# Pooled attention between MLP matmuls: scores in 64x64 PE tiles, AV in 64-row tiles, four bursts a batch, k and v loaded by halves of 64 partitions

## The chip, the cores and the metric

The kernel runs on one core of one Trainium2 chip. The metric is the time of one execution on the device in microseconds (us), as the median of several executions. A ratio below is computed as the mean time of one kernel's fast runs over the mean time of the other's fast runs in the same rounds on the same chip, so it is not quite the ratio of the medians that are quoted. An execution is called disturbed, and left out of the ratios, when it is more than 1.5% above the fastest of the same kernel.

Engine names in the profile: PE is TensorE (matmuls), PEld its weight loads, DVE is VectorE, ACT is ScalarE, POOL is GpSimd, SP is SyncE. SPq and ACTq are those engines' sequencers, which also issue DMAs. A DMA "lands" when all its data has arrived. Its landing is told by a semaphore, a counter on which the instructions that need the data wait.

## The reference

```python
def _attn_ref(q, k, v):                       # each 8 x 8 heads x 576 x 64, float32
    k_p = k.reshape(B, H, 72, 8, D).mean(axis=3)     # 576 keys pooled to 72
    v_p = v.reshape(B, H, 72, 8, D).mean(axis=3)
    scores = scale * np.matmul(q, k_p.transpose(0, 1, 3, 2))
    attn = softmax(scores)                    # cut: max, exp, sum
    return np.matmul(attn, v_p)
def _moe_ref(x, w_in, w_out):                 # x: 4608 x 512; w_in 512 x 2048; w_out 2048 x 512
    h = x @ w_in
    g = h - np.tanh(h)
    return g @ w_out
# reference(): x is the attention output with heads side by side, then the MLP
```

## The kernel before

The MLP dominates. Its 4608 rows are done in nine groups of 512: `mlp_h` (h = x w_in, 64 matmuls of 512 columns) and then `mlp_o` (64 more). The attention of batch b+1 is put between the `mlp_o` matmuls of group b, so for six groups (the "stream") TensorE alternates between the two. Batches 0 and 1 are done in the start of the program.

A head has 72 pooled keys, so two heads make 144 rows: 128 go on the partitions of one tile, 16 are left over. K and v come in as raw rows of 8 x 64 floats (2 KB), are pooled by POOL, and k is transposed by a DMA.

```python
def load_main(src, dst, b, t0, t1):           # 128 partitions, four tiles, 1 MB
    return nc.sync.dma_start(out=dst[:, t0:t1, :], in_=src[b, 0:128, t0:t1, :])

def score_mms(b, t, dst, c0, c1, ...):        # two heads in one matmul: KB is block-diagonal
    ... nc.tensor.matmul(dst[p : p + w], lhsT=KB[b % 2][:, o : o + w], rhs=qTs[b][:, m, c0:c1], ...)

def av_half(b, blk, half, x_sb, alloc):       # three matmuls of 130 columns, 128 rows
    for n in range(3): ...
        nc.tensor.matmul(..., lhsT=E[:, t, c0 : c0 + 128], rhs=vb[:, s0 : s0 + 2, :], ...)

for g in range(1, NG):                        # the stream
    for i in range(NHID):
        mlp_h(g, i, gts)
        ...                                   # i == 0: POOL pools k and v of batch nb
        if i == (3 if g == 1 else 8):
            k_dma_transpose(nb); k_place(nb, nc.gpsimd.tensor_copy)
            load_k(nb + 1); load_v(nb + 1); load_q(nb + 1)      # all on one queue, SP's
    for tb in range(4):
        for qd in range(4):
            mlp_o(g, tb, qd * 4, qd * 4 + 4, gts)               # four o_ps matmuls
            u = tb * 4 + qd
            if 1 <= u <= NT: scores(nb, u - 1)
            if u in (7, 8, 9, 10, 12): av(nb, ..., True)        # x goes to xT by DMA transposes
            if u == 12: q_cast(nb + 1); q_dma_transpose(nb + 1)
```

The first `mlp_h` matmul of group b+1 needs xT (x transposed) of batch b+1, which is written by the DMA transposes of that batch's AV.

The softmax here doesn't subtract the row's maximum and nothing guards it: scores larger than these inputs give would overflow.

## Time and profile before

| | before |
|---|---|
| median, in the first rounds | 301.89 us (300.75 to 302.37, 4 runs) |
| span of the profiled run | 299.1 us |
| PE busy | 97% |
| granted TensorE clock | 1.00 |
| first stream group starts | 54.98 us |
| a streaming batch | 30.80 us |
| bytes moved by DMA | 49.79 MB |

The page's view by engine, the stretches of the stream and the order of instructions are shown in the prediction.

### The profile page before, as it was taken

To read this page: it belongs to the slowest core of one execution; us is meant where nothing else is said; L and a number is where in the kernel's file an instruction comes from. 1 tells how busy PE (TensorE), PEld (TensorE's weight loads), DVE (VectorE), ACT (ScalarE), POOL (GpSimd) and SP (SyncE) were. 2 spreads that over 40 slices of the span, in tenths; PEclk is the share of its full clock that TensorE was granted. 3 is DMA by queue.
4 is the path that set the end of the run, shared out by engine and by line. 5 is a ranking of instruction groups with operands and counts; after the bars stand their busy time and mean duration, and the time that the engine had idled before them with its cause. 6 is when DMAs were issued, how large, how long until landed. Compare 5 with 4: busy or idle time off the path is not lost.

```text
span 299.1 us, 4694 instructions
## 1 busy us (share of the span) xinstructions
PE 291.5 (97%) x1671; PEld 142.5 (48%) x1671; DVE 159.1 (53%) x343; ACT 149.4 (50%) x283; POOL 115.5 (39%) x110
## 2 busy tenths in 40 slices
PE   7989999999999999999999999999999999999994
PEld 3454455544544454445444554455445544444443
DVE  5658665673547444753476247716680758108600
ACT  4647583666146633654265516650665166126511
POOL 8500904871496109922971089307940000000000
PEclk9999999999999999999999999999999999999999
DMA  7999999849854998699648974897431430111032
GB/s 251 226 211 278 311 227 310 263 87 328 234 113 99 271 297 134 117 302 245 107 88 235 300 167 94 242 294 159 97 66 35 95 92 0 37 70 36 0 72 70
DMA packets 66183, 49.79 MB, mean 166 GB/s; under 512 B 39920, under 2 KB 52976, under 8 KB 66160
## 3 DMA queue, kind: packets, MB, share of 16 engines
q1 hardware_dynamic: 58832, 42.94, 56.0%
q0 software_dynamic: 4752, 4.72, 9.4%
q10 hardware_dynamic: 2576, 1.84, 2.3%
q8 instruction: 13, 0.21, 0.3%
q14 instruction: 10, 0.08, 0.1%
HBM read 36.70 MB, written 9.44 MB: 154 GB/s over the span
## 4 chain that ended last, share of the span: by engine, by line
PE 85%; DMA 9%; POOL 4%; issue 0%; SPq 0%; ACT 0%; DVE 0%; POOLq 0%
PE o_ps L456 40%; PE hT_ps L428 37%; DMA w1b<-in_moe_w_in_dram 4%; PE x_ps L346 4%; DMA k_raw<-in_k_dram 4%; PE s_ps L298 3%; POOL k_raw L198 1%; DMA out_dram<-o_sb 1%; POOL k_raw L203 1%; POOL kd L206 1%; POOL w2b L510 0%; PE xT_ps L390 0%; POOL v_raw L576 0%; PE qT_ps L171 0%; POOL w1b L503 0%
## 5 line engine op out<-in xcount | busy, mean ns | idle before, releaser
L456 PE MATMUL o_ps<-w2b,gT 128*128 128x512 bf16 x560 | 134.4, 380 | 0.0
L441 DVE TENSOR_TENSOR gT<-hT_ps,t_sb 128x512 bf16<-128x512 f32 x144 | 98.9, 691 | 57.7 <-ACT t_sb L439 57.6
L428 PE MATMUL hT_ps<-xT,w1b 128*128 128x512 bf16 x576 | 126.9, 379 | 0.3 <-ACT xT L397 0.3
L439 ACT ACTIVATE t_sb<-hT_ps 128x512 f32<-128x512 f32 x144 | 85.6, 597 | 38.3 <-PE hT_ps L428 37.5
L428 PEld LDWEIGHTS <-w1b 128*128 128x128 bf16 x576 | 55.9, 98 | 66.5 <-issue 0.4
L456 PEld LDWEIGHTS <-gT 128*128 128x128 bf16 x560 | 52.5, 98 | 52.0 <-issue 1.4
L465 ACT COPY o_sb<-o_ps 128x512 f32<-128x512 f32 x33 | 19.3, 585 | 75.2 <-PE o_ps L456 75.2
L359 DVE RECIPROCAL rden<-x_ps 128x4 f32<-128x4 f32 x80 | 14.2, 177 | 52.5 <-PE x_ps L346 52.0
L360 DVE TENSOR_TENSOR x_sb<-x_ps,rden 128x256 bf16<-128x256 f32 x80 | 34.0, 425 | 3.5 <-DMA xT<-x_sb 0.6
L148 POOL CAST q_bf<-q_raw 128x2048 bf16<-128x2048 f32 x6 | 11.3, 1888 | 59.9 <-issue 34.8
L198 POOL TENSOR_TENSOR k_raw<-k_raw 128x1280 f32<-128x1280 f32 x7 | 20.2, 2886 | 27.4 <-DMA k_raw<-in_k_dram 16.6
L317 ACT ACTIVATE E<-s_ps 128x288 bf16<-128x288 f32 x60 | 21.4, 410 | 13.2 <-PE s_ps L298 13.0
L346 PE MATMUL x_ps<-VB,E 128*128 128x130 bf16 x240 | 20.8, 221 | 0.4 <-ACT xT L397 0.3
L346 PEld LDWEIGHTS <-E 128*128 128x128 bf16 x240 | 16.9, 98 | 8.8 <-DVE VB L230 0.6
L216 POOL TENSOR_TENSOR v_raw<-v_raw 128x1280 f32<-128x1280 f32 x6 | 17.4, 2898 | 0.0
L298 PE MATMUL s_ps<-qT,KB 128*128 128x288 bf16 (+5 forms) x128 | 17.0, 290 | 0.2
L298 PEld LDWEIGHTS <-KB 128*128 128x128 bf16 (+1 forms) x128 | 7.0, 96 | 10.2 <-issue 3.5
L527 PE MATMUL warm_ps<-xT 128*128 128x512 bf16 x29 | 10.2, 465 | 1.3 <-DVE xT L539 1.3
L206 POOL TENSOR_TENSOR kd<-k_raw 128x640 bf16<-128x640 f32 x7 | 10.8, 1540 | 0.5
L203 POOL TENSOR_TENSOR k_raw<-k_raw 128x640 f32<-128x640 f32 x7 | 10.8, 1541 | 0.5
L397 ACT CAST xT<-xT_ps 128x256 bf16<-128x256 f32 (+1 forms) x14 | 5.8, 436 | 8.5 <-PE xT_ps L390 5.1
L219 POOL TENSOR_TENSOR v_raw<-v_raw 128x640 f32<-128x640 f32 x6 | 9.3, 1544 | 0.5
(73 smaller groups left out, 100.7 us busy)
## 6 DMA issues: line engine op xcount, KB each, us to landing
k_raw<-in_k_dram SPq DMA_DIRECT2D x7, 1024.0 KB, 5.9
q_raw<-in_q_dram SPq DMA_DIRECT2D x7, 1024.0 KB, 10.2
v_raw<-in_v_dram SPq DMA_DIRECT2D x7, 1024.0 KB, 9.3
out_dram<-o_sb SPq DMA_DIRECT2D x38, 128.0 KB, 2.4
out_dram<-o_sb SPq DMA_DIRECT2D x16, 256.0 KB, 3.7
w1b<-in_moe_w_in_dram POOLq DMA_DIRECT2D x4, 512.0 KB, 14.2
w2b<-in_moe_w_out_dram POOLq DMA_DIRECT2D x4, 512.0 KB, 16.9
k_raw<-in_k_dram SPq DMA_DIRECT2D x7, 128.0 KB, 5.8
```

The lines of the kernel that those rows point to most:

```text
L198: first = eng.tensor_tensor(out=r[:, :, 0:4, :], in0=r[:, :, 0:4, :], in1=r[:, :, 4:8, :], op=ALU.add)
L216: eng.tensor_tensor(out=r[:, :, 0:4, :], in0=r[:, :, 0:4, :], in1=r[:, :, 4:8, :], op=ALU.add)
L298: nc.tensor.matmul(dst[p : p + w], lhsT=KB[b % 2][:, o : o + w], rhs=qTs[b][:, m, c0:c1], start=True, stop=True,)
L317: nc.scalar.activation(out=E[:, t, half * hs : (half + 1) * hs], in_=ps[:, :], func=ACT.Exp, scale=SCALE)
L346: nc.tensor.matmul(ps[:, 2 * n : 2 * n + 2, :].rearrange("p h d -> p (h d)") if n < 2 else ps.rearrange("p (a s) d -> p a s d", s=2)[:, :, ...
L359: nc.vector.reciprocal(out=rden[:, :, :], in_=ps[:, :, D:D1])
L360: nc.vector.tensor_tensor(out=x_sb[:, half, :, :], in0=ps[:, :, 0:D], in1=rden[:, :, :].to_broadcast([128, 4, D]), op=ALU.mult,)
L428: nc.tensor.matmul(h_tiles[i][:, :], lhsT=w1b[:, fb, i * 128 : (i + 1) * 128], rhs=xT[:, fb, tok0 : tok0 + TG], start=(fb == 0), stop=(fb ...
L439: nc.scalar.activation(out=t_sb[:, :], in_=h_ps[:, :], func=ACT.Tanh)
L441: nc.vector.tensor_sub(out=gT[:, :], in0=h_ps[:, :], in1=t_sb[:, :])
L456: nc.tensor.matmul(o_ps[:, :], lhsT=gts[i][:, tb * 128 : (tb + 1) * 128], rhs=w2b[:, i, :], start=(i == 0), stop=(i == NHID - 1),)
L465: (nc.vector.tensor_copy if g == 0 and tb % 2 else nc.scalar.copy)(out=o_sb[:, :], in_=o_ps[:, :])
```

## The change

The intent: block-diagonal k wastes half of each score matmul on zeros, and AV multiplies with masked v. In tiles of the PE array (64x64 for scores, 64 rows x 128 columns for AV) four or two small matmuls run at a time and nothing is multiplied by zero. Since a change of tile shape costs time, the small matmuls are grouped in four bursts a batch (before: ten), which needs six PSUM banks at once. For the tiles the layout of pooled k and v must be: head pair's first head on partitions 0 to 63, second on 64 to 127. So k and v are loaded by two DMAs of 64 neighbouring partitions each.

```diff
-    def load_main(src, dst, b, t0, t1):
-        return nc.sync.dma_start(out=dst[:, t0:t1, :], in_=src[b, 0:128, t0:t1, :])
+    def load_half(src, dst, b, i, ts=slice(0, NM), eng=nc.sync):
+        return eng.dma_start(out=dst[64 * i : 64 * i + 64, ts, :], in_=src[b, i, :, ts, :])
+
+    def load_main(src, dst, b):
+        return [load_half(src, dst, b, i) for i in range(2)]
 ... (cut: banks by hand, left-over rows in one load, masks)
+    def score_main(b, j, dst, c0, c1):
+        for s, i in ((0, 0), (1, 1), (0, 1), (1, 0)):
+            m = j + 2 * i
+            nc.tensor.matmul(
+                dst[s][64 * i : 64 * i + 64],
+                lhsT=kTs[b][64 * s : 64 * s + 64, m, 64 * s : 64 * s + 64],
+                rhs=qTs[b][64 * s : 64 * s + 64, m, c0:c1],
 ... (cut)
+    def av_mms(b, blk, pss):
+        mms = [(pss[i][:, t, :], i, t, vb[64 * i : 64 * i + 64, t, :])
+            for t in range(NM) for i in range(2)
+        ] + [...]                                   # one more pair, 260 columns, left-over rows
+        for n, (dst, i, t, rhs) in enumerate(mms):
+            nc.tensor.matmul(dst, lhsT=E[64 * i : 64 * i + 64, t, c0 : c0 + 128], rhs=rhs, ...)
 ... (cut: the start, reordered for scores of four heads at once)
-                    if 1 <= u <= NT:
-                        scores(nb, u - 1)
-                    if u in (7, 8, 9, 10, 12):
-                        av(nb, (7, 8, 9, 10, 12).index(u), ps_b1, True)
+                    if u in (2, 5):
+                        scores_pairs(nb, u // 3)
+                    if u in (7, 10):
+                        av_stream(nb, (0, 1, 2) if u == 7 else (3, 4))
```

## The prediction

> **What bounds the kernel now.** I read the page first, then the busy time of each engine over chosen stretches, then the instructions in order of time, at last the list of waits. The page says that TensorE is busy 97% of the span, and that its two MLP lines make most of the chain that ended last:
>
> ```profile
> PE 291.5 (97%) x1671; PEld 142.5 (48%) x1671; DVE 159.1 (53%) x343; ACT 149.4 (50%) x283; POOL 115.5 (39%) x110
> ...
> L456 PE MATMUL o_ps<-w2b,gT 128*128 128x512 bf16 x560 | 134.4, 380 | 0.0
> L428 PE MATMUL hT_ps<-xT,w1b 128*128 128x512 bf16 x576 | 126.9, 379 | 0.3 <-ACT xT L397 0.3
> L346 PE MATMUL x_ps<-VB,E 128*128 128x130 bf16 x240 | 20.8, 221 | 0.4 <-ACT xT L397 0.3
> ```
>
> To be seen: the idle time before the MLP groups (last column) is nothing, while DVE, ACT and POOL are about half idle. A busy sum is not yet a limit, so I compared one streaming batch (an MLP group with the attention of the next batch put between its o_ps matmuls) with an MLP group at the end that has no attention in it:
>
> ```profile
> 85.95:116.75 30.80, 30.80 (x175) 15.07 (x174) 16.68 (x36) 15.36 (x30) 13.73 (x12) 1.00 0.86 202
> 116.75:147.56 30.81, 30.81 (x176) 15.05 (x174) 16.68 (x36) 15.36 (x30) 19.11 (x16) 1.00 0.77 186
> 239.98:267.61 27.63, 27.63 (x130) 12.50 (x128) 11.07 (x16) 11.89 (x20) 0.00 (x0) 1.00 0.16 50
> ```
>
> The columns are the stretch, its length, then busy time of PE, PEld, DVE, ACT, POOL, the clock, the DMA share and GB/s. The difference, 30.80 - 27.63 = 3.17 us, is all that attention costs on TensorE in one of the six streaming batches. 6 x 3.17 = 19.0 us is the whole pot for the stream. In order of time, where that 3.17 goes in one batch:
>
> ```profile
> 73.84 0.41 PE L298 MATMUL s_ps<-qT,KB 128*128 128x288 bf16 x2
> 74.09 1.03 PE L456 MATMUL o_ps<-w2b,gT 128*128 128x512 bf16 x4
> 75.04 0.43 PE L298 MATMUL s_ps<-qT,KB 128*32 128x288 bf16 x8
> 75.41 1.90 PE L456 MATMUL o_ps<-w2b,gT 128*128 128x512 bf16 x8
> 77.14 0.51 PE L346 MATMUL x_ps<-VB,E 128*128 128x130 bf16 x6
> 77.49 1.03 PE L456 MATMUL o_ps<-w2b,gT 128*128 128x512 bf16 x4
> ```
>
> First column start, second duration with the last one's latency. What counts is start to start. One o_ps matmul takes 0.216 us. Two score matmuls of 288 columns take 0.25 (73.84 to 74.09), six AV matmuls of 130 columns 0.35 (77.14 to 77.49). The left-over scores (8 matmuls in 32-column tiles) take 0.46: four o_ps matmuls from 74.09 would have ended their stream at 74.95, and the next starts at 75.41. Sum: 4 x 0.25 + 0.46 + 5 x 0.35 = 3.2, the 3.17 found above.
>
> The left-over scores are the one place before where tiles are used. In the single records four of them start within 10 ns (75.044 to 75.054), the other four 123 ns later, so four tiles do run as one. But the first starts 310 ns after the o_ps matmul ahead of it (not 216), and the next o_ps 219 ns after the last of them (not some 120). So one change of tile shape costs about 0.095 us, in and out alike.
>
> The third place is the start of the program, up to 55 us, where TensorE is not always the bound:
>
> ```profile
> 30.21 2.90 POOL L198 TENSOR_TENSOR k_raw<-k_raw 128x1280 f32<-128x1280 f32 x1 [16.58 <-DMA k_raw<-in_k_dram]
> ...
> 36.23 1.54 POOL L206 TENSOR_TENSOR kd<-k_raw 128x640 bf16<-128x640 f32 x1
> ...
> 37.82 0.45 PE L259 MATMUL kT_ps<-ident,kd 128*128 128x128 bf16 x5 [0.52 <-POOL kd L206]
> ```
>
> POOL waits 16.6 us for k of batch 1, pools it, and TensorE waits (0.5 us; its weight load 1.0) for the result. So TensorE's own start (the MLP's h matmuls run without a break from 20.4) is already as fast as that chain lets it be, bar about half a microsecond.
>
> **What the Trainium skill says.** "TensorEngine Tiling (Array Packing)", Key Properties: changing the tiling mode drains TensorE; the trace agrees, 0.095 us each way. "TensorE: Matmul & The Clock Gate", Part 3: matmuls in different tiles start some 4 ns apart and finish as one; the trace agrees for 32-column tiles (2 to 5 ns). The same page, Weight-path perf modes: the fast weight load wants 128 weight columns. Before, N = 64 matmuls that each load 128 columns follow each other 28 to 30 ns apart, so such a load takes no more than that; nothing before shows 64-row or 64x64 tiles. "DMA: Bandwidth & Descriptors", Queues: engines take turns between queues; so splitting a load into two on one queue adds no bandwidth.
>
> **The change part by part.** From the built order of the changed kernel, a streaming batch has four bursts between o_ps matmuls instead of ten.
> - Main scores: 8 matmuls of 128x288 become 16 in 64x64 tiles, four at a time: 4 x 0.123 = 0.49 in place of 1.0.
> - Left-over scores: the same 8 matmuls, 2 x 0.123 = 0.25.
> - AV: per block six matmuls of 130 columns (0.35) become four pairs of 65 columns and one pair of 260, each pair in two 64-row tiles. A pair of 65 columns takes at least 0.03 (the N = 64 pace above), the 260 one 260/512 x 0.216 = 0.11: 0.23 a block if pairs run as one, 0.35 if the two weight loads follow each other (0.06 a pair). The latter is no gain at all. I take 0.25.
> - Changes of shape: two before. After: burst 1 has three (in, 64x64 to 32 columns, out), the others two each: nine, 9 x 0.1 = 0.9 in place of 0.2.
>
> Sum after: 0.49 + 0.25 + 5 x 0.25 + 0.9 = 2.89 against 3.17: **0.28 us saved a batch, 1.7 us for six**. All of it is on the path, since TensorE is idle nowhere in that stretch.
>
> What moves beside it. ACT: ten exponentials of 288 columns (410 ns each) become five of 576 (about 0.65 by the step from 410 at 288 to 597 at 512), so 4.1 to 3.3 us. DVE: ten reciprocals of 177 and ten products of 425 ns become five pairs of some 0.2 and 0.69, 6.0 to 4.5 us. POOL: placing k and one wide mask go. All of these engines are half idle, so this is worth nothing in itself. Six banks a burst can make waits, so I checked the tightest: AV's first burst needs the exponentials of burst 2, 2 x 0.65 + some 0.3 after TensorE leaves, and eight o_ps matmuls (1.73) lie between. Just enough.
>
> Start. Whole-block AV (four times 0.2 + 0.69 on DVE instead of eight times 0.6), no copy of v's left rows by POOL, and scores of four heads per load should make the MLP's first matmuls start some 2 us earlier than now (an estimate from the rows of DVE: 19.6 now). But w1 and k of batch 1 come over DMA engines that are saturated (share 1.24 between 10 and 20 us), and the same bytes are wanted. K of batch 1 is issued when the second piece of w1 lands (18.7), lands at 30.05, and POOL needs 7.7 us for it. POOL issues w1 perhaps 0.5 us sooner. So the 2 us turn into a longer wait at the k transpose near 37 us, and about **0.4 us** is left.
>
> Batch 1 and the end of batch 0 use AV block by block with two changes of shape each: 0.25 + 0.2 against 0.35, so six times +0.1, less 0.2 for the scores: **+0.4 us**, of which the part in batch 0 goes into the wait.
>
> Sum: -1.7 - 0.4 + 0.3 = -1.8, so 302.1 - 1.8 = **300.3 us**.
>
> **Rivals.** (a) The bursts save nothing: row tiles with a 128-column weight load each don't pair up, AV stays at 0.35 a block, and the changes of shape eat the scores' gain. Then a batch costs 0.49 + 0.25 + 1.75 + 0.9 = 3.39, 6 x 0.22 = +1.3 us, and 303 us in all. For it: no 64-row tile was seen before. Against it: 32-column tiles load their weights 3 ns apart. I give it one chance in five. (b) The start does get faster: smaller loads by halves make k of batch 1 or w1 land earlier, and the 2 us count in full: 298.5. For it: less on the queues' issue (v's left rows in one load, not four). Against: saturated DMA, and loads of 64 partitions that fill from one queue may rather be slower. One in six. (c) Waits: the exponentials or the norms don't end in time for the next burst, some 0.3 us a batch: 302. The lists of waits before have no TensorE wait at all between 60 and 240 us, and the new order leaves slack everywhere but in one place. (d) Transfers in the stream: k and v split in two and landing later. They have many microseconds of slack there (k of the next batch lands at 72, and is pooled from 85.95 on), so nothing.
>
> **Range and chances.** AV's pace moves the result by +2.5 or -0.6 us, the start by +1 or -2, waits by +1.5. Low 298.4, high 302.9. Faster by over 2% needs 296.1 us, a saving of 6.0: stream and start together at their best give some 4.5. Slower by over 2% needs a stall of one microsecond in every batch. So 0.03, 0.94, 0.03.
>
> **What would show it.** A streaming batch of 30.5 us in place of 30.80; three to five tenths between o_ps matmuls at the second burst, 0.8 at the first, about 0.95 at the third; four score matmuls starting within some 15 ns; AV pairs about 30 ns apart (60 would be rival a). h matmuls from about 17 to 18 us, and a wait of 2 to 3 us at the k transpose of batch 1 near 37.5. Wrong it would be if that transpose starts before 36 or after 39, if TensorE waits inside a batch for ACT or DVE, or if a pair of AV matmuls takes over 45 ns.

## More of the kernel before

From the page of the kernel before, the queue that carries the loads and the median time of its loads from issue to landing:

```profile
q1 hardware_dynamic: 58832, 42.94, 56.0%
...
k_raw<-in_k_dram SPq DMA_DIRECT2D x7, 1024.0 KB, 5.9
q_raw<-in_q_dram SPq DMA_DIRECT2D x7, 1024.0 KB, 10.2
v_raw<-in_v_dram SPq DMA_DIRECT2D x7, 1024.0 KB, 9.3
```

Columns of the first line: packets, megabytes, and the time those packets took as a share of 16 engines' span. Then the same kernel's stretches from the first MLP matmul to the stream, and over the four middle streaming batches:

```profile
18.49:54.98 36.49, 35.65 (x252) 18.73 (x252) 23.68 (x54) 23.23 (x43) 13.44 (x8) 1.00 1.12 275
85.78:209.01 123.23, 123.23 (x697) 60.23 (x696) 66.70 (x144) 61.42 (x120) 63.30 (x51) 1.00 0.80 195
```

After the engines' busy times come the clock, the DMA share and GB/s. (A share above 1 means that packet durations overlap.) In the start the DMA engines are full, at 1.12. In the stream they are at 0.80 on average.

## The result

| | before | after |
|---|---|---|
| median | 301.89 us (4 runs) | 329.77 us (329.60 to 331.58, 4 runs) |
| ratio | | 1.0943, 95% interval 1.0893 to 1.0993 |
| span of the profiled run | 299.1 us | 327.9 us |
| granted TensorE clock | 1.00 | 0.969 |
| first stream group starts | 54.98 us | 63.18 us |
| six streaming batches | 184.84 us | 205.82 us |
| from there to the end | 59.3 us | 58.9 us |

The result is correct and 9.4% slower. The predicted time was 300.3 us, and the range ended at 302.9. The last three rows split the 28.8 us by which the span grew: +8.2 in the start, +21.0 in the stream, -0.4 at the end.

The page after, the lines of engines, the clock and DMA by slice, and the chain that ended last:

```profile
PE 296.9 (91%) x1881; PEld 135.9 (41%) x1916; DVE 148.2 (45%) x270; ACT 145.2 (44%) x251; POOL 105.7 (32%) x96
...
PEclk9799979999796999989999999999999999999999
DMA  7999999984998599969995899479963162021023
...
PE 67%; DMA 23%; SPq 3%; issue 2%; POOL 2%; DVE 1%; ACT 1%; POOLq 0%
PE PS L477 34%; PE PS L506 28%; DMA q_raw<-in_q_dram 11%; DMA xT<-x_sb 7%; DMA w1b<-in_moe_w_in_dram 4%; PE PS L377 2%; PE PS L308 1%; SPq L127 1%; DMA out_dram<-o_sb 1%; PE PS L318 1%; ACT q_bf L166 1%; SPq L133 1%; DVE x_sb L412 0%; POOL v_raw L127 0%; SPq L293 0%
```

PE was 97% busy and is now 91%. The chain was PE 85% and is now PE 67%, DMA 23%. In the chain, `q_raw` loads have 11% and the transposes of x 7%; neither was among the first entries before. The clock dips in some of the slices in which PE idled or just after them, not in all.

The MLP groups of the same page, and the DMA lines that answer to those of before:

```profile
L477 PE MATMUL PS<-xT,w1b 128*128 128x512 bf16 (+1 forms) x586 | 129.9, 379 | 15.0 <-DMA xT<-x_sb 13.0
L506 PE MATMUL PS<-w2b,gT 128*128 128x512 bf16 x537 | 128.4, 385 | 2.3 <-issue 1.6
...
q1 hardware_dynamic: 59040, 43.07, 64.6%
...
k_raw<-in_k_dram SPq DMA_DIRECT2D x14, 512.0 KB, 7.3
v_raw<-in_v_dram SPq DMA_DIRECT2D x14, 512.0 KB, 9.8
q_raw<-in_q_dram SPq DMA_DIRECT2D x5, 1024.0 KB, 15.4
```

The matmuls themselves are a little slower: told apart by shape, those of 512 columns take 387 and 385 ns, and 379 and 380 before. (The 379 in the first line is a mean with 40 shorter ones in it.) The h matmuls have 15 us of idle time before them where they had 0.3, and 13.0 of it ended with a transpose of x. The queue moves 43.07 MB instead of 42.94, but its packets take 64.6% of a longer span instead of 56.0%. A load of 512 KB of k now lands after 7.3 us; one of 1024 KB landed after 5.9 us. The q loads of 1024 KB are what they were before, and land after 15.4 us instead of 10.2: they are issued on the same queue behind k and v.

The stretches after, from the start of one h phase to the next:

```profile
22.36:63.18 40.82, 37.64 (x301) 19.59 (x306) 22.89 (x52) 22.78 (x43) 10.75 (x7) 0.96 1.09 204
63.18:103.04 39.86, 32.18 (x201) 13.98 (x203) 15.94 (x27) 15.12 (x26) 14.56 (x13) 0.92 0.90 192
103.04:138.09 35.05, 32.33 (x198) 14.08 (x203) 15.29 (x26) 14.75 (x25) 14.84 (x12) 0.94 0.89 170
138.09:171.60 33.51, 31.99 (x199) 14.03 (x203) 15.29 (x26) 14.75 (x25) 15.14 (x12) 0.95 0.94 178
171.60:204.37 32.77, 30.39 (x199) 13.62 (x204) 15.29 (x26) 14.75 (x25) 13.68 (x12) 1.00 0.89 179
204.37:238.45 34.08, 30.39 (x199) 13.61 (x203) 15.29 (x26) 14.75 (x25) 14.29 (x11) 1.00 0.89 174
238.45:269.00 30.55, 30.23 (x199) 13.71 (x204) 15.29 (x26) 14.17 (x24) 12.63 (x10) 1.00 0.44 85
103.04:238.45 135.41, 125.11 (x793) 55.35 (x809) 61.14 (x104) 58.99 (x100) 57.95 (x44) 0.97 0.90 175
```

The first five streaming batches take 33 to 40 us at a DMA share of 0.89 to 0.94. The sixth, which has no further batch to load (share 0.44), takes 30.55: 0.25 less than before. So the change is worth on PE what was predicted, wherever the loads let it. In the start, the share of 1.09 is much that of before (1.12), but it moved 204 GB/s instead of 275.

How a slow load becomes a PE wait is seen in the chain of the longest one, in order of time (start, duration, what):

```profile
83.77 0.62 SPq L133
84.39 0.04 issue
84.43 15.36 DMA q_raw<-in_q_dram
99.86 3.04 DMA xT<-x_sb
102.90 0.14 issue
103.04 1.01 PE PS L477 x2
```

The q load is issued at 84.43, at the end of the row of k and v loads, and takes 15.36 us. The transpose of x that the profile chains to it is issued at 99.86, though the norms that feed the transposes had all started by 94.2. In the trace's instruction records the two use the same semaphore (number 104), and SP waits on it before it issues the later one. So x doesn't need the data of q: the transpose waits for q because semaphores are used again in turn. It lands at 102.90, and 0.14 us later the first h matmul of the next group starts, 5.3 us late.

The packets behind this, from the trace: on that queue, a packet of 2 KB (a row of k or v, or of the output) had a median duration of 84 ns before and has 154 ns after (means 107.1 and 146.9, over 12,992 and 12,800 packets).

**What page of the Trainium skill bears on it.** The page "SBUF — State Buffer", section "Door 1: The DMA port swizzle (why `[64,N]` ≈ `[32,N]`)", says that partitions 0 to 63 reach only 8 of 16 ports to SBUF and 64 to 127 the other 8; it gives 196 GB/s against 328 for a transfer of 1 MiB, a factor of 0.60. The packets are near it: 84/154 = 0.55. The prediction had not looked this page up.

### The profile page after: what moved, and what is told of

It is laid out like the page before. It is cut to its first block, busy times and chain, and to the rows that moved or that the text cites. A ratio compares the mean times of both kernels' runs of the same rounds, so it can differ in the third digit from the quotient of the medians.

```text
span 327.9 us, 5052 instructions
## 1 busy us (share of the span) xinstructions
PE 296.9 (91%) x1881; PEld 135.9 (41%) x1916; DVE 148.2 (45%) x270; ACT 145.2 (44%) x251; POOL 105.7 (32%) x96
## 3 DMA queue, kind: packets, MB, share of 16 engines
q1 hardware_dynamic: 59040, 43.07, 64.6%
## 4 chain that ended last, share of the span: by engine, by line
PE 67%; DMA 23%; SPq 3%; issue 2%; POOL 2%; DVE 1%; ACT 1%; POOLq 0%
PE PS L477 34%; PE PS L506 28%; DMA q_raw<-in_q_dram 11%; DMA xT<-x_sb 7%; DMA w1b<-in_moe_w_in_dram 4%; PE PS L377 2%; PE PS L308 1%; SPq L127 1%; DMA out_dram<-o_sb 1%; PE PS L318 1%; ACT q_bf L166 1%; SPq L133 1%; DVE x_sb L412 0%; POOL v_raw L127 0%; SPq L293 0%
## 5 line engine op out<-in xcount | busy, mean ns | idle before, releaser
L477 PE MATMUL PS<-xT,w1b 128*128 128x512 bf16 (+1 forms) x586 | 129.9, 379 | 15.0 <-DMA xT<-x_sb 13.0
L491 DVE TENSOR_TENSOR gT<-PS,t_sb 128x512 bf16<-128x512 f32 x144 | 99.0, 691 | 83.9 <-ACT t_sb L489 83.0
L506 PE MATMUL PS<-w2b,gT 128*128 128x512 bf16 x537 | 128.4, 385 | 2.3 <-issue 1.6
L489 ACT ACTIVATE t_sb<-PS 128x512 f32<-128x512 f32 x144 | 85.9, 599 | 57.1 <-PE PS L477 55.6
L515 ACT COPY o_sb<-PS 128x512 f32<-128x512 f32 x33 | 19.5, 590 | 69.7 <-PE PS L506 69.7
L327 ACT ACTIVATE E<-PS 128x576 bf16<-128x576 f32 (+3 forms) x44 | 23.9, 606 | 28.2 <-PE PS L308 27.3
L412 DVE TENSOR_TENSOR x_sb<-PS,rden 128x512 bf16<-128x512 f32 x30 | 20.8, 692 | 1.0
L575 PE MATMUL PS<-xT 128*128 128x512 bf16 x28 | 10.6, 504 | 1.2 <-DVE xT L587 1.2
L377 PE MATMUL PS<-VB,E 64*128 64x65 bf16 x320 | 11.3, 192 | 0.0
L377 PE MATMUL PS<-VL,E 64*128 64x260 bf16 x80 | 10.2, 268 | 0.1
## 6 DMA issues: line engine op xcount, KB each, us to landing
q_raw<-in_q_dram SPq DMA_DIRECT2D x5, 1024.0 KB, 15.4
```

What stands on the lines that cost most here:

```text
L327: nc.scalar.activation(out=out, in_=in_, func=ACT.Exp, scale=SCALE)
L377: nc.tensor.matmul(dst, lhsT=E[64 * i : 64 * i + 64, t, c0 : c0 + 128], rhs=rhs, start=(n < 2), stop=(n >= len(mms) - 2), skip_group_check ...
L412: nc.vector.tensor_tensor(out=out, in0=ps[:, :, :, 0:D], in1=rden[:, :, :, :].to_broadcast([128, 2, NM, D]), op=ALU.mult,)
L477: nc.tensor.matmul(h_tiles[i][:, c0:c1], lhsT=w1b[:, fb, i * 128 : (i + 1) * 128], rhs=xT[:, fb, tok0 + c0 : tok0 + c1], start=(fb == 0 an ...
L489: nc.scalar.activation(out=t_sb[:, :], in_=h_ps[:, :], func=ACT.Tanh)
L491: nc.vector.tensor_sub(out=gT[:, :], in0=h_ps[:, :], in1=t_sb[:, :])
```

## The experiments

Theory, formed after the result: the loads of 64 neighbouring partitions are the whole of the loss; PE's part of the change is as good as predicted. Rivals: the tiles or bursts cost something that only shows in the stream; splitting a load in two costs, whatever the partitions; the lost clock is a cause of its own; the start alone is at fault.

All medians (those of e3, e5 and e8 have one disturbed run in them; the ratios don't), in the order of their rounds; each ratio is to the kernel before in the same rounds (300.66, 300.76, 300.72 and 300.87 us):

| run | median us | ratio [95%] |
|---|---|---|
| e1 after, full-width loads | 300.56 | 0.9994 [0.9976, 1.0013] |
| e2 before, halves of 64 | 322.00 | 1.0698 [1.0674, 1.0723] |
| e3 before, every other partition | 315.98 | 1.0486 [1.0415, 1.0558] |
| e4 after, halves on two queues | 350.00 | 1.1643 [1.1619, 1.1666] |
| e5 before, halves, stream only | 313.20 | 1.0391 [1.0359, 1.0423] |
| e6 before, every other, stream only | 300.90 | 1.0001 [0.9983, 1.0019] |
| e7 after, full width in the stream only | 307.73 | 1.0229 [1.0194, 1.0265] |
| e8 after, mended | 302.80 | 1.0059 [1.0041, 1.0077] |
| e9 after, idle time filled | 328.10 | 1.0897 [1.0876, 1.0919] |
| e10 e1 without bursts for AV | 304.31 | 1.0125 [1.0104, 1.0147] |
| e11 before, only k in halves, stream | 302.18 | 1.0045 [1.0030, 1.0061] |
| e12 start of before, stream of e8 | 300.06 | 0.9979 [0.9963, 0.9996] |
| e13 before, only v in halves, stream | 303.18 | 1.0076 [1.0050, 1.0103] |
| e14 e5 again, one look | 314.42 | (one run) |

### e1: the changed kernel with full-width loads

The same bytes in the same number of DMAs, but each load has two of the four tiles over all 128 partitions. The rows land in wrong places, so the result is wrong (relative error 1.30). Instructions, sizes and counts are those of the changed kernel.

```diff
     def load_half(src, dst, b, i, ts=slice(0, NM), eng=nc.sync):
-        return eng.dma_start(out=dst[64 * i : 64 * i + 64, ts, :], in_=src[b, i, :, ts, :])
+        return eng.dma_start(out=dst[:, 2 * i : 2 * i + 2, :], in_=flat[b, 0:128, 2 * i : 2 * i + 2, :])
 ... (cut: one tile per load in the start)
```

> The changed kernel with the same number of loads of k and v and the same bytes, but every load over all 128 partitions (two of the four tiles a load, instead of 64 partitions of all four). The rows then lie in wrong places, so the result is wrong on purpose. Theory P (loads into 64 neighbouring partitions move at half the rate, and the late loads hold up everything behind them on the queue): 298 to 303 us, 2 KB packets back at a median near 84 ns (154 in the changed kernel), no wait of TensorE inside a streaming batch, clock back at 1.0. Rival B (the four bursts, the grouped transposes of x or the reuse of banks make the waits): stays at 325 to 332 us.

Measured 300.56 us. The median 2 KB packet is 84 ns again. PE waits nowhere in the stream, as the stretches show (start; first streaming batch; the four middle ones):

```profile
20.07:56.52 36.45, 36.16 (x305) 19.34 (x305) 22.85 (x52) 22.74 (x43) 13.43 (x8) 1.00 1.08 275
56.52:87.07 30.55, 30.55 (x205) 13.69 (x202) 15.92 (x27) 14.51 (x25) 13.53 (x11) 1.00 0.84 200
87.07:209.27 122.20, 122.20 (x810) 54.75 (x808) 61.08 (x104) 58.91 (x100) 59.79 (x46) 1.00 0.78 196
```

Busy time equals the length: 30.55 us a batch. So tiles, bursts and banks are innocent, and the width of the loads is the whole loss of 29 us. This run also lets the prediction's sum for PE be read in one batch (start, duration with the last one's latency, what):

```profile
73.01 0.44 PE L318 MATMUL PS<-qT,kT 64*64 64x288 bf16 x8
73.38 0.43 PE L328 MATMUL PS<-qT,KL 128*32 128x288 bf16 x8
73.74 2.77 PE L516 MATMUL PS<-w2b,gT 128*128 128x512 bf16 x12
76.44 0.44 PE L318 MATMUL PS<-qT,kT 64*64 64x288 bf16 x8
76.81 1.90 PE L516 MATMUL PS<-w2b,gT 128*128 128x512 bf16 x8
78.64 0.30 PE L387 MATMUL PS<-VB,E 64*128 64x65 bf16 x8
78.78 0.27 PE L387 MATMUL PS<-VL,E 64*128 64x260 bf16 x2
78.89 0.29 PE L387 MATMUL PS<-VB,E 64*128 64x65 bf16 x8
...
79.46 2.76 PE L516 MATMUL PS<-w2b,gT 128*128 128x512 bf16 x12
```

As in the prediction, what counts is start to start at 0.216 us an o_ps matmul. The last o_ps before this stretch starts at 72.705 and would have made way at 72.92; the next starts at 73.74, so burst 1 cost 0.82 us. Burst 2 lies between 76.33 (73.74 plus twelve matmuls) and 76.81: 0.48. The third lies between 78.54 and 79.46: 0.92. The fourth, which ends with the o_ps matmul at 82.74, is 0.69. The sum is 2.91 us; predicted was 2.89. A pair of 65-column AV matmuls starts 29 to 39 ns after the last, and its two halves 2 to 5 ns apart.

### e2 and e3: the kernel before with its loads split

e2 splits each main load of the kernel before into two of 64 neighbouring partitions, e3 into two of every other partition. All else stays, results are correct.

```diff
 # e2 (e3: slice(i, 128, 2) in place of slice(64 * i, 64 * i + 64))
-        return nc.sync.dma_start(out=dst[:, t0:t1, :], in_=src[b, 0:128, t0:t1, :])
+        return [
+            nc.sync.dma_start(out=dst[slice(64 * i, 64 * i + 64), t0:t1, :],
+                in_=src[b, slice(64 * i, 64 * i + 64), t0:t1, :])
+            for i in range(2)
+        ]
```

> The kernel before with one thing changed: each main load of k and v (from the SP queue) is two loads of 64 neighbouring partitions. Right result. Theory P: slower, 312 to 330 us, 2 KB packets at a median near 154 ns. Rival B: 302, at most 304 us for the additional issues.

> As the run before, but each of the two loads takes every other partition (0, 2, 4 ... and 1, 3, 5 ...), so again 64 partitions a load. Right result. If it is the ports that a load reaches (theory P as the SBUF page has it): 301 to 304 us and packets near 84 ns. If it is the number of partitions or of loads: as slow as the run before.

Measured 322.00 and 315.98 us (313.92 without its disturbed run), so e3 missed the 301 to 304 us that were expected of it. The packets separate the two cleanly: a median of 154 ns in e2, of 84 in e3. So do the four middle batches of the stream:

```profile
102.40:232.94 130.54, 123.90 (x697) 60.07 (x697) 65.68 (x141) 61.55 (x121) 62.38 (x52) 1.00 0.89 181
```

```profile
99.03:222.25 123.22, 123.22 (x697) 60.29 (x696) 66.61 (x144) 61.42 (x120) 63.61 (x53) 1.00 0.79 195
```

e2 (first) takes 130.5 us there, e3 (second) 123.2, as the kernel before. But both lose in the start, 15.9 and 13.2 us by the first stream group, and e3 has no slow packets. The cause is in ACT's timeline of e2, a line that e3 has too (9.06 us):

```profile
31.67 0.92 ACT L400 CAST xT<-xT_ps 128x256 bf16<-128x256 f32 x3 [9.88 <-DMA k_raw<-in_k_dram]
```

ACT sat idle for 9.88 us, until a k load had landed: its own sequencer stood at the issue of a DMA of q, which waits for a semaphore of a load on the other queue. More loads in flight at the start made that collision. So neither start tells anything of the changed kernel, and both runs were inconclusive there.

### e4: the halves on two queues

If the two halves ran side by side they would fill all ports. The changed kernel, with each second half issued from ACT:

```diff
-        return [load_half(src, dst, b, i) for i in range(2)]
+        return [load_half(src, dst, b, i, eng=(nc.sync, nc.scalar)[i]) for i in range(2)]
```

> The changed kernel with the second half of each streamed k and v load on the ScalarE queue, the first half on SP. Right result. If two halves in flight at once fill both sets of ports: 300 to 312 us. If, as the SBUF page says, two loads can't be fused: within 2% of the changed kernel, 323 to 333 us; a further cost is possible from the issues on ScalarE.

Measured 350.00 us, worse than anything else and outside both expected ranges. The packets of 2 KB stay slow (medians 148 and 144 ns on the two queues). On top, PE waits 22.2 us in the stream for gT, the product of DVE that needs ACT's tanh: ACT is now held at its DMA issues (16.4 us of its waits before tanh end with a DMA). The same page of the skill, section "Can I just issue two DMAs to hit both halves?", says no, with +6% for two at once. This run agrees that it is no remedy, though it doesn't measure that figure.

### e5 and e6: as e2 and e3, but in the stream only

```diff
+        if b < 2:
+            return [nc.sync.dma_start(out=dst[:, t0:t1, :], in_=src[b, 0:128, t0:t1, :])]
```

> The kernel before with only the streamed loads (batch 2 and later) of k and v split into two loads of 64 neighbouring partitions; the start is untouched, because in the two runs before this the split at the start also shifted which load waits for which semaphore and held up ScalarE by 10 us. Right result. Theory P, ports: the streaming part of the earlier run grew by 7.9 us, so 306 to 311 us. Rival, the number of loads: the same as the even and odd run of this call.

> As the run before, with every other partition in each of the two loads. Theory P, ports: 299 to 302 us, as the kernel before. Rival, the number of partitions or of loads: as slow as the run before.

Measured 313.20 (313.01 without its disturbed run) and 300.90 us; 306 to 311 was expected of e5, so the size was missed by 2 us. This is the cleanest pair: the kernel before, correct results, the same number of loads, the same bytes, the same queue. Neighbouring partitions cost some 12 us, every other partition nothing. So "two loads instead of one" is not the cause, and 64 partitions are not either; it matters which 64. The profiled execution of e5 was disturbed (1084 us); its other three runs agree (311.6 to 313.4).

### e7: the changed kernel, full width in the stream only

```diff
+        if b < 2:
+            return eng.dma_start(out=dst[64 * i : 64 * i + 64, ts, :], in_=src[b, i, :, ts, :])
```

(ahead of e1's form; wrong as there.)

> The changed kernel with full-width loads only from batch 2 on, the start as changed (64 neighbouring partitions). Wrong result on purpose. If the loss adds up of the start (stream begins 8.2 us later in the changed kernel, 1.5 us later with full-width loads everywhere) and of the stream: 305 to 310 us. If the backlog of the start is what spoils the stream: over 312 us.

Measured 307.73 us. From the first h matmul to the stream it is as slow as the changed kernel; the middle batches are at full pace:

```profile
22.16:63.49 41.33, 38.17 (x305) 19.74 (x305) 22.88 (x52) 22.76 (x43) 13.41 (x8) 0.96 1.10 238
94.32:216.52 122.20, 122.20 (x808) 54.80 (x809) 61.15 (x104) 58.85 (x100) 59.24 (x45) 1.00 0.81 196
```

The stream starts at 63.49, against 56.52 in e1: the halves cost 7.0 us in the start. The rest, some 22 us (329.8 - 307.7), is the stream. So both parts are due to the same loads, and the start alone was not at fault.

### e9: the idle time filled

In the changed kernel TensorE idles, and the granted clock falls afterwards. To tell whether that adds its own time, dummy matmuls were put where it idles most.

```diff
+                    if g == 1 and u == 2:
+                        warm_pe(9, b0=5)
 ...
+                    if g in (1, 2) and u == 15:
+                        warm_pe(22 if g == 1 else 10, b0=5)
```

> The changed kernel, with idle stretches of TensorE in group 1 and 2 of the first heads filled by dummy matmuls into a bank that is free then. Theory (the loads set the pace and the lost clock is only a companion): the time stays within 1.5 us of the changed kernel's 329.8, the mean granted clock goes up from 0.969. Rival (the clock that falls after the idle stretches adds its own microseconds, about 5 of the 28): about 324 us.

Measured 328.10 us, by the ratios some 1.4 us less than the changed kernel (1.0897 against 1.0943), with the clock at 0.983. The four middle batches:

```profile
103.47:236.97 133.50, 126.69 (x819) 55.92 (x819) 61.11 (x104) 58.98 (x100) 57.80 (x44) 0.99 0.91 178
```

133.5 us, against 135.4, at nearly the same DMA share. The rival's 324 us did not come. But only about half of the lost clock was given back, and 1.4 us is within the intervals of the two ratios, so this run bounds the clock's own part loosely. Another bound: over the six streaming batches PE is busy for 187.52 us in the changed kernel and 183.30 in e1. The slower matmuls are thus worth 4.2 us at most; the rest of the loss there is waiting.

### e11, e13 and e14: how much slow loading the stream can bear

The kernel before, with k alone, v alone, or both in halves of 64 neighbours, from batch 2 on.

```diff
 # e11 (e13: v_pairs in place of k_pairs; e14: without that condition, as e5)
+        if b < 2 or src is not k_pairs:
+            return [nc.sync.dma_start(out=dst[:, t0:t1, :], in_=src[b, 0:128, t0:t1, :])]
```

> The kernel before, with only the k loads of batches 2 to 5 as two loads of 64 neighbouring partitions; v and q as before. With both k and v (and q) so, the stream cost 12 us. Theory (the queue had slack, and the loss begins only once the slower packets fill the queue's whole batch): at most 303 us. Rival (each slow load delays its consumer by itself): near half of the loss, 306 to 307.

> The kernel before, with only the v loads of batches 2 to 5 as two loads of 64 neighbouring partitions. With k alone it was 302.18 (+1.5), with both some +12. Theory (there is a fixed amount of room on the DMA engines, and either tensor alone just fits into it): as with k alone, 302 to 303.5, and a DMA share near 0.87 in the four middle batches. Rival (v is what hurts, because the q load queued behind it is the one that is waited for): 308 to 312, most of the loss.

> Both k and v of batches 2 to 5 by halves of 64 partitions, in the kernel before: one look, because the profiled execution of the first run of this form was disturbed (1084 us) and left no usable trace. Theory (room runs out): about 312 us, DMA share of 0.90 or more in the batches that got longer, each of them ending in a wait of the first MLP matmul for a transposed x. Rival (each load delays its own consumer, with the engines not full): the same time, with a DMA share no higher than with k alone, 0.87.

Measured +1.5, +2.3 and, with both, +12 to +13.6 us. The four middle batches of each, in that order (of e14 also the first streaming batch and the first of the four):

```profile
87.08:210.32 123.24, 123.23 (x696) 60.35 (x697) 66.64 (x144) 60.87 (x119) 64.53 (x53) 1.00 0.87 194
```

```profile
87.55:211.12 123.57, 123.40 (x697) 60.23 (x698) 66.65 (x144) 60.87 (x119) 65.00 (x53) 1.00 0.89 194
```

```profile
54.71:93.12 38.41, 31.14 (x176) 15.02 (x174) 17.31 (x37) 15.73 (x31) 16.29 (x15) 0.98 0.93 199
93.12:126.56 33.44, 33.44 (x175) 15.68 (x175) 16.66 (x36) 14.77 (x29) 16.39 (x14) 0.92 0.85 178
93.12:222.96 129.84, 126.35 (x697) 60.66 (x696) 65.69 (x141) 61.42 (x120) 63.11 (x52) 0.98 0.90 182
```

Length times DMA share is the work of the DMA engines, here for one batch: 24.6 us before (123.23 x 0.80 / 4), 26.8 with k, 27.5 with v, 29.2 with both, and 30.5 in the changed kernel (135.41 x 0.90 / 4). The step from before to both, 4.6 us, is what the packets make of it: two tensors of 512 packets, each 70 ns longer, over 16 engines are 4.5 us. With v alone the share is 0.89 and the batches still take the 30.8 to 30.9 us that PE needs; with either tensor alone, what is lost is lost for the most part in the first streaming batch (32.5 and 32.3 us). With more work the share hardly rises, 0.90, and the batch grows instead, to 129.84/4 = 32.5 us. No streaming batch of these runs or of the changed kernel shows a share above 0.94. So the loss is not k's or v's own: each alone nearly fits, and the two together don't. Both rivals (half the loss with k; v in particular) fall.

Two things in e14 are not as expected. Over half of its loss, 7.6 us, is in the first streaming batch. And one of the four that follow (33.44 us) has no wait of PE at all: PE is busy throughout, at a clock of 0.92 and a DMA share of 0.85. That batch grew by its clock; the other three grew by 1.0 to 1.7 us at shares of 0.90 to 0.92.

### e10: what the bursts are worth

e1 (wrong), with AV of each of the five blocks in a burst of its own: six more changes of shape a batch.

```diff
-                    if u in (7, 10):
-                        av_stream(nb, (0, 1, 2) if u == 7 else (3, 4))
+                    if u in (7, 8, 9, 10, 12):
+                        blk = (7, 8, 9, 10, 12).index(u)
+                        av_stream(nb, (blk,), ((6, 0, 4)[blk % 3],))
```

> The full-width form of the changed kernel (300.56 us; wrong data on purpose), with AV of each block in its own step again, so that a batch has six more changes of tile shape. Theory (a change of shape drains the array and costs about 0.1 us): 6 x 0.1 x 6 batches = +3.6 us, so about 304. Rival (a change of shape costs nothing beside the matmuls; the grouping in bursts buys nothing): 300.6, within 0.6.

Measured 304.31 us. Its batches are 31.18 to 31.19 us, against 30.55: 0.635 us for six changes, 0.106 each. Without the bursts the tiles would be slower than the kernel before (30.80), so the grouping is needed for the change to be worth anything.

### e8: a mended version

If every other partition is as fast as full width, then the changed kernel can keep its tiles: half i of k goes to partitions i, i+2, i+4, ..., score weights are picked with a stride of two, and v is brought into halves by one matmul with a permutation matrix for each batch.

```diff
-        return eng.dma_start(out=dst[64 * i : 64 * i + 64, ts, :], in_=src[b, i, :, ts, :])
+        return eng.dma_start(out=dst[i::2, ts, :], in_=src[b, i, :, ts, :])
 ...
-                lhsT=kTs[b][64 * s : 64 * s + 64, m, 64 * s : 64 * s + 64],
+                lhsT=kTs[b][64 * s : 64 * s + 64, m, s::2],
 ...
+    def v_perm(b, ps):
+        nc.tensor.matmul(ps, lhsT=perm[:, :], rhs=VP[b % 2].rearrange("p t d -> p (t d)"), ...)
+        nc.vector.tensor_copy(out=VB[b % 2][:, :, 0:D], in_=ps.rearrange("p (t d) -> p t d", t=NM))
```

> A mended version with a right result: each half of k and v goes to every other partition (all ports); the score matmuls take every other column of k transposed as weights, and v is brought to 64 neighbouring partitions by one permutation matmul of 256 columns a batch. Theory P: 298 to 303 us (300.6 with full-width loads, and 6 x 0.11 us for the permutation). Rival B: stays above 320 us.

Correct, and 302.62 us in its three undisturbed runs (302.39 to 302.98; the 302.80 above has the disturbed one in it). That undoes all but some 2 us of the loss, but it is 0.6% slower than the kernel before. Its profiled execution was a disturbed one (clock 0.755).

### e12: the start of before, the stream of e8

Batches 0 and 1 and their loads as in the kernel before, the stream as in e8.

```diff
     def load_k(b):
+        if b > 1:
+            return load_wide(k_main, k_raw[b % 2], b) + load_rest(k_left, k_raw[b % 2], b)
 ... (cut: the same for v; scores_pairs, av_stream and v_perm of e8 in the stream loop)
```

> A correct kernel: batches 0 and 1 as in the kernel before (full-width loads, its scores), batches 2 to 5 in the changed form with loads to every other partition and one permutation matmul a batch for v. Theory (the PE side of the change saves 0.25 us a batch, the permutation gives 0.11 back, the start is that of before): 0.5 to 0.9 us less than before, 299.7 to 300.2. Rival (a switch of forms in mid-stream, or the two halves of a load, brings a new wait): 301 or more.

Correct, 300.06 us (six runs), 0.9979 of the kernel before, and the interval ends below 1. Three of its batches:

```profile
55.45:86.10 30.65, 30.65 (x205) 13.79 (x203) 16.35 (x28) 14.51 (x25) 14.74 (x13) 1.00 0.71 206
86.10:116.76 30.66, 30.66 (x204) 13.82 (x203) 15.71 (x27) 14.72 (x25) 14.30 (x11) 1.00 0.79 193
116.76:147.42 30.66, 30.66 (x204) 13.80 (x203) 15.71 (x27) 14.72 (x25) 15.89 (x13) 1.00 0.70 196
```

30.66 us is 30.55 and 0.11 for the permutation, as expected; six of them save 0.84 us, and the stream starts 0.47 us later than before (55.45). The gain is tiny, 0.6 us of 300.7: the interval just excludes no gain.

## Why the prediction was wrong

**The step that failed** is rival (d), "k and v split in two and landing later. They have many microseconds of slack there ..., so nothing", with the sentence under the skill that "splitting a load into two on one queue adds no bandwidth" as the whole account of the loads by halves. What the runs showed in its place: a 2 KB packet to 64 neighbouring partitions takes 154 ns, not 84, and the stream has too little slack for that. It cost 12 to 13.6 us with k and v so loaded in the stream of the kernel before (e5, e14), and 22.5 us in the stream of the changed one. It adds 4.6 us of DMA work to a batch (e14). The room, as an estimate from the shares, was 0.10 x 30.8 = 3.1 us (0.80 before, about 0.90 where batches grew).

The prediction looked at the slack of one load, when k lands against when it is pooled, and read it too wide: k is not pooled from 85.95 on but from 81.27, when POOL is done with its cast of q, and that cast had waited for q (the timeline of POOL in the kernel before):

```profile
78.85 1.89 POOL L148 CAST q_bf<-q_raw 128x2048 bf16<-128x2048 f32 x1 [10.68 <-DMA q_raw<-in_q_dram]
81.27 2.88 POOL L198 TENSOR_TENSOR k_raw<-k_raw 128x1280 f32<-128x1280 f32 x1
```

What counted was the loads' common queue. The load that ended late was q, behind k and v, and the wait was for a transpose of x that uses q's semaphore again. The kernel before has the same reuse: in its first four streaming batches q landed 4.1, 1.4, 5.9 and 2.6 us before that transpose was issued (from the instruction records of its trace). These few microseconds were the slack. The prediction did name loads of 64 partitions, under rival (b): they "may rather be slower". It held that against a gain and never priced it. That was the place to look up the page on SBUF, and to multiply.

Point by point:

- *PE's sum.* Right. Predicted 2.89 us for what attention costs in a batch, measured 2.91 in one batch of e1; a batch of 30.52 (30.80 - 0.28) against 30.55 in e1 and in the last streaming batch of the changed kernel itself. Six of them save 1.5 us (predicted 1.7).
- *Changes of shape*, 0.095 read and 0.1 used: 0.106 measured (e10). Right.
- *Rival (a)*, AV pairs that don't run as pairs: ruled out, pairs start 29 to 39 ns after one another (e1).
- *Rival (c)*, waits for ACT or DVE: none. The tightest place, AV's first burst, has no wait in e1.
- *The start*, predicted -0.4, and h matmuls from "about 17 to 18 us". Wrong by its sign even without the halves: in e1 the first h matmul starts at 20.07, before at 18.49, and the stream at 56.52 instead of 54.98, +1.5 us (this has the +0.3 of batches 0 and 1 in it). The first scores need two tiles of k and q of four heads, where one tile and two heads did; the first k transpose starts at 6.32 us in e1 and at 5.07 before. The foretold wait at the k transpose of batch 1 did not come. With the measured start the predicted change of -1.8 us (-1.7 - 0.4 + 0.3) would have been -1.7 + 1.5 = -0.2, well inside the range; e1 measured -0.1 (300.56 beside 300.66). The prediction also starts from 302.1 us, where the median is 301.89.
- *The sum.* The span grew by 28.8 us: +1.5 for the start as such, +6.7 for halves in the start (63.18 - 56.52), -1.5 for PE in the stream, +22.5 for halves in the stream (205.82 - 183.30), -0.4 at the end, whose cause was not looked into. 29.2 of it is the one term that was put at nothing.

Of the 22.5 us in the stream, the list of waits has 13.0 for transposes of x and 2.1 for the transpose of k. Most of the rest, 4.2 us, is slower matmuls after idle times.

That the loads of 64 neighbouring partitions cause the loss is shown (e1, e5, e6). How they lengthen a batch is in part argued. Lack of room on the DMA engines fits the shares. But the share in the start reached 1.12, so 0.90 is no ceiling of the engines, and a share of 0.89 still fitted with v alone. A chain fits too: a late q holds up SP's queue by the semaphores and POOL's pooling of the next k and v, and so the next loads. No run gave the transposes semaphores or a queue of their own, so the two are not told apart.

Open too is what makes e8 some 2.5 us slower than e12 (302.62 and 300.06). Their streams are written the same, so by difference it is in e8's start. About 1.1 of it is the changed start as e1 shows it (56.52, and 55.45 in e12); no usable trace shows the rest.

## What to carry to other kernels

When a change alters a load's layout, price its packets, not only its bytes, and add up all DMA work of a steady period. The slack of one load says little: here the wait came in a transfer that did not even need the late load's data. If a layout wants the two halves of the partitions apart, load them to every other partition and pay for the order elsewhere, here 0.11 us a batch for a permutation matmul, instead of loading 64 neighbours. And when a change mixes a gain on one engine with a new layout of transfers, test each alone first; here the gain was real (1.5 us in the stream) and the layout cost 29.2.

## What the Trainium skill lacked or had wrong

- "SBUF — State Buffer", "Door 1": agrees on 64 neighbouring partitions (its 0.60 of the full rate; 84/154 = 0.55 here). It lacks what follows from its own formula for strides: 64 partitions taken as every other one run at full rate, 84 ns for a packet of 2 KB and 300.90 us for the kernel (e6).
- The same page, "Can I just issue two DMAs to hit both halves?": its sentence that the only way to reach all 16 ports is one transfer spanning all 128 partitions leaves that form out; by e6 two loads of 64 partitions each (300.90 us, packets of 84 ns) are as good as one of 128, if each has every other partition.
- "TensorEngine Tiling (Array Packing)", Key Properties, says that a change of tiling mode drains TensorE, with no number: here 0.106 us each (e10).
- No page that I found gives a figure for how long an engine can be held at the issue of a DMA that waits for another load: ACT stood for 9.88 us at the issue of a q load (e2). With half of the k and v loads issued from ACT the kernel was 6% slower still (e4, 350.0 us against 329.8).
- No page that I found gives the share of DMA time up to which a steady stream keeps its pace: here it held with 0.89 (e13), three batches grew at 0.90 to 0.92 (e14), and no streaming batch went above 0.94.
